# Two transformer layers on one core: weights split once and kept in DRAM as parts, later early maxima, another delay of the row transposes, and normalised outputs in two blocks per chunk

## The chip, the cores and the metric

The kernel runs on one core of a Trainium2 chip. Its engines work side by side: PE (matrix products), DVE (vector work), ACT (functions, and a DMA queue of its own), POOL (slower vector work) and SP (issues most DMAs). The metric is the device time of one execution in microseconds, as a median over runs.

## What is computed

Two equal layers, each an attention block and an MLP with the Mish function, on x of 2048 rows by 512, 32 heads of 16, hidden width 1792. All inputs are float32, and both layers use the same weights.

```python
    def _A_ref(x, wqkv, wo):
        ...
        scores = jnp.einsum("bhqd,bhkd->bhqk", q, k) * (Dh ** -0.5)
        p = _softmax(scores, axis=-1)
        o = jnp.einsum("bhqk,bhkd->bhqd", p, v)
        return (lambda x, *d: x.transpose(*d))(o, 0, 2, 1, 3).reshape(B, S, D) @ wo
    def _B_ref(x, w1, b1, w2):
        h = jnp.einsum("bsd,df->bsf", x, w1) + b1
        sp = jnp.log1p(jnp.exp(-jnp.abs(h))) + jnp.where(h > 0, h, jnp.zeros_like(h))  # stable softplus
        act = h * jnp.tanh(sp)
        return jnp.einsum("bsf,fd->bsd", act, w2)
    x = A_x
    x = x + _A_ref(_layernorm(x, axis=-1), A_wqkv, A_wo)
    x = x + _B_ref(_layernorm(x, axis=-1), B_w1, B_b1, B_w2)
    x = x + _A_ref(_layernorm(x, axis=-1), A_wqkv, A_wo)
    x = x + _B_ref(_layernorm(x, axis=-1), B_w1, B_b1, B_w2)
    return x
```

## The kernel before

**Numbers in two parts.** A float32 operand is split into a rounded part (hi, fp32r) and the rest (lo), and each product is three matmuls (mm3, L136 to L141): hi by hi, hi by lo, lo by hi. A weight block of 0.5 MB is loaded as raw float32 and split into a 1 MB tile of both parts (split_load, L104 to L124): the load on SP's queue (L110) or ACT's (L108), the rounding on ACT, POOL or DVE (L114, L116), the subtraction on POOL or DVE (L118). There are 22 such blocks: 6 of wqkv, 2 of wo, 7 of w1, 7 of w2. Each layer loads and splits all of them again.

**Memory.** Most tiles share one pool of 22 blocks of 8 KB per partition (blk): weights, residuals x2, normed inputs, keys ks, queries qs, values va, probabilities p, and the attention's outputs. A pool of small tiles has the tags raw (3 buffers, raw weights and pt), f (2 buffers: xn, ot, hb), he, hr and others. A tile waits until the last reader of what was in its buffer is done.

**Projections** (qkv, L400 to L464). The 2048 rows are four chunks c of 512. An order of 36 units, (m, c), is worked off: 32 of queries and keys (12 matmuls each, result split into pt and written to DRAM as scr by ACT's queue, L446) and four of values (48 matmuls each, vscr). When the units that the first head group needs are through, SP loads ks and qs for it, 24 loads of 128 KB (prep_qk). From the third unit after that (start, L454; the unit of index 12 in layer 0 and 11 in layer 1), 24 steps of early maxima (AHEAD) are interleaved, one behind each unit or each quarter of a value unit.

**Attention** (run, L366 to L391). 512 steps; a step is one key tile of 128 for four heads and 512 queries. Its work is a fixed order per two steps, CYCLE: Q is two heads' scores (PE matmul L322, exponential on ACT L324), X one score and one row maximum (PE L242, DVE L275), M a pair of maxima (DVE L260), v the product with the values (PE L348). Maxima run 24 steps ahead, since a block's maxima are subtracted inside the score matmul by two extra rows of qs. When 16 steps of maxima are complete, DVE folds them (L282), POOL splits the result (nh, L287 and L288), DVE transposes it (L296) and SP carries it through DRAM into qs (max_rows). The transpose is put on a list with a delay (L289), which tick counts down. When the maxima are through (step 488), the order is TAIL. Each Order chains the instructions that it is given on each engine in the order written; what is not chained (weights, heads, loads) is placed by the framework's scheduler.

**Attention's end and boundary.** After each 16 steps ACT copies a block of outputs to ot (L361), and SP writes its sums and rows to DRAM. heads (L466 to L483) normalises a chunk: load the sums, reciprocal on DVE (L470), write it to DRAM spread over the rows (inv), load raw outputs (oraw) and inverses (rall), and multiply: hi on DVE (L480), the same product again on POOL (L481), lo on DVE (L482). It takes four blocks. heads(0) and (1) are hooked into the attention's last steps, (2) and (3) follow it. project (L485 to L496) multiplies with wo, and DVE adds the residual; then comes a layernorm of chunk 0, and the MLP (hid and outp, hid two ahead). wo is split on POOL in the attention's last group; w1 and w2 are loaded and split around the projections.

Of the kernel before, what the change touches and what calls it, by code (L numbers as in the profile page):

```python
# [50 lines left out]
def kernel(ctx: ExitStack, tc: tile.TileContext, x, wqkv, wo, w1, b1, w2, out):  # L51
# [52 lines left out]
    def split_load(src, a, b, name, hi="act", lo="pool", behind=False, later=None):  # L104
        t = b8([P, 2, a, b], F32R, name)
        raw = tmp.tile([P, a, b], F32, tag="raw", name=name + "r", bufs=3)
        if behind:
            tc.keep_in_program_order(nc.scalar.dma_start(raw, src))  # L108
        else:
            nc.sync.dma_start(raw, src)  # L110

        def split():
# [5 lines left out]
            eng.tensor_tensor(t[:, 1], raw, t[:, 0].bitcast(F32), op=ALU.subtract)  # L118

# [6 lines left out]
    def load_cols(w, j, name, **kw):  # L126
        return split_load(w[:, ts(j, 2 * P)].rearrange("(k p) n -> p k n", p=P), KT, 2 * P, name, **kw)

    def load_rows(w, j, name, **kw):
        return split_load(w[ts(j, 2 * P), :].rearrange("(k p) n -> p k n", p=P), 2, w.shape[1], name, **kw)  # L130
# [335 lines left out]
    def heads(att, c):  # L466
# [9 lines left out]
        nc.sync.dma_start(r, inv.rearrange("h d q -> (h d) q").rearrange("(k p) q -> p k q", p=P))  # L476
        oh = b8([P, KT, CW], F32R, f"oh{l}{c}")
        ol = b8([P, KT, CW], F32R, f"ol{l}{c}")
        for k in range(KT):
            nc.vector.tensor_tensor(oh[:, k], o[:, k], r[:, k], op=ALU.mult)  # L480
            nc.gpsimd.tensor_tensor(o[:, k], o[:, k], r[:, k], op=ALU.mult)  # L481
# [195 lines left out]
```

## Time and profile before

| what | us |
|---|---|
| median of 3 runs (lowest, highest) | 3735.68 (3728.65, 3739.83) |
| the profiled execution's time | 3735.5 |
| span of that execution, first to last instruction | 3733.7 |
| busy: PE, DVE, ACT, POOL | 3518.1, 3096.8, 2564.1, 521.5 |
| mean granted clock of PE | 0.973 |
| layer 0: first matmul of the projection with wo, first h matmul of the MLP | 1464.75, 1539.04 |
| layer 1: first h matmul of the MLP | 3401.67 |

A row of a timeline gives start and length in us, engine, line, operation, output and inputs, and in brackets how long the engine stood idle before it and for what. A row of groups gives the count, busy us and mean ns, and the idle time ahead of the group's instructions with what ended it. A row of the busy table gives for a stretch each engine's busy us and count, the granted clock, the DMA engines' busy share and GB/s. Matmul ends are modelled, so a count of matmuls says more of PE's pace than its busy time.

### The profile page before, as it was taken

What the parts mean: (1) busy time and instruction counts of PE and PEld (TensorE: products, weight loads), DVE (VectorE), ACT (ScalarE), POOL (GpSimd) and SP (SyncE); (2) the same over time, 40 slices, a digit from 0 to 9 for tenths busy, and PEclk for the clock granted to TensorE, in tenths of its full rate; (3) what the DMA queues carried; (4) which work ended last, traced back from release to release, by engine and by line L of the source; (5) the groups of instructions that cost most, each with busy time, mean ns of one, the idle gap of its engine ahead of it and who ended that gap; (6) DMA issues with size and microseconds to landing.
All of it is one profiled execution on the core that took longest, in us unless ns stands there. A gap on an engine that the chain in (4) does not pass through costs nothing.

```text
span 3733.7 us, 70993 instructions
## 1 busy us (share of the span) xinstructions
PE 3518.1 (94%) x29056; PEld 1936.2 (52%) x29056; DVE 3096.8 (83%) x4150; ACT 2564.1 (69%) x4787; POOL 521.5 (14%) x465
## 2 busy tenths in 40 slices
PE   5999999999999988799979999999999999887999
PEld 4654444444444434577757444444444444346787
DVE  4679999999999984766646899999999999856555
ACT  2168888888888875244421788888888888742444
POOL 2000000000000002645410000000000000035444
PEclk8999999999999998899989999999999999888999
DMA  6440211202112015100045402112021120151000
GB/s 187 153 107 21 52 23 35 50 8 51 26 32 51 18 29 173 52 12 12 29 136 170 103 9 51 26 32 51 7 51 33 25 52 17 30 173 51 12 12 23
DMA packets 131894, 203.85 MB, mean 55 GB/s; under 512 B 28656, under 2 KB 73712, under 8 KB 123376
## 3 DMA queue, kind: packets, MB, share of 16 engines
q1 hardware_dynamic: 109872, 159.46, 18.3%
q10 hardware_dynamic: 21696, 39.85, 2.9%
q8 instruction: 228, 3.74, 0.4%
q14 instruction: 98, 0.80, 0.1%
HBM read 121.12 MB, written 77.07 MB: 53 GB/s over the span
## 4 chain that ended last, share of the span: by engine, by line
DVE 67%; PE 17%; POOL 5%; DMA 4%; ACT 3%; issue 2%; SPq 0%; ACTq 0%; POOLq 0%; DVEq 0%
DVE mxv L275 29%; DVE mxv L260 28%; PE pv L348 3%; POOL hb L520 2%; PE sp L322 2%; DVE al L521 2%; PE qk L139 1%; POOL hb L517 1%; DVE he L512 1%; PE qk L141 1%; PE qk L140 1%; DVE ah L519 1%; DMA rall<-inv 1%; DVE he L514 1%; PE va L139 1%
## 5 line engine op out<-in xcount | busy, mean ns | idle before, releaser
L324 ACT ACTIVATE p<-sp 128x512 f32<-128x512 f32 x4096 | 2134.1, 599 | 348.0 <-PE pn L242 206.1
L275 DVE TENSOR_REDUCE mxv<-pn 128x1 f32<-128x512 f32 x2048 | 1323.1, 694 | 27.9 <-PE pn L242 27.1
L260 DVE TENSOR_REDUCE mxv<-pm 128x2 f32<-128x1024 f32 x1024 | 1260.9, 1231 | 78.5 <-PE pm L242 78.0
L322 PE MATMUL sp<-qs,ks 50*128 50x512 f32 x4096 | 1298.0, 450 | 27.0 <-ACT p L324 26.7
L348 PE MATMUL pv<-p,va 128*32 128x256 f32 x16384 | 1209.0, 391 | 0.0
L322 PEld LDWEIGHTS sp<-qs,ks 50*128 50x128 f32 x4096 | 573.3, 185 | 745.8 <-ACT p L324 628.3
L242 PE MATMUL pn<-ks,qs 48*128 48x512 f32 x2048 | 825.0, 451 | 70.6 <-DVE mxv L275 53.2
L348 PEld LDWEIGHTS pv<-p,va 128*32 128x32 f32 x16384 | 380.6, 109 | 555.3 <-issue 441.5
L242 PE MATMUL pm<-ks,qs 48*128 48x512 f32 x2048 | 439.6, 423 | 22.8 <-DMA ks<-scr 16.7
L242 PEld LDWEIGHTS pn<-ks,qs 48*128 48x128 f32 x2048 | 366.9, 184 | 94.9 <-DVE mxv L275 76.6
L287 POOL CAST nh<-nm 128x16 fp32r<-128x16 f32 x64 | 12.7, 198 | 2638.9 <-DVE nm L282 2638.9
L242 PEld LDWEIGHTS pm<-ks,qs 48*128 48x128 f32 x2048 | 195.1, 186 | 86.2 <-DMA ks<-scr 18.0
L139 PE MATMUL mo<-w,ah 128*128 128x512 f32 x448 | 178.7, 399 | 11.0 <-DVE ah L519 7.9
L517 POOL TENSOR_TENSOR hb<-hb,he 128x512 f32<-128x512 f32 x112 | 158.2, 1413 | 183.3 <-DVE he L514 179.1
L521 DVE TENSOR_TENSOR al<-hb,ah 128x512 fp32r<-128x512 f32 x112 | 108.3, 967 | 90.0 <-POOL hb L520 88.8
L520 POOL TENSOR_TENSOR hb<-hb,hr 128x512 f32<-128x512 f32 x112 | 160.8, 1435 | 132.7 <-DVE ah L519 129.4
L139 PE MATMUL h<-thm,w 128*128 128x512 f32 x448 | 177.5, 398 | 1.6 <-ACT thm L133 1.6
L140 PE MATMUL h<-tlm,w 128*128 128x512 f32 x448 | 176.9, 395 | 0.0
L141 PE MATMUL h<-thm,w 128*128 128x512 f32 x448 | 176.8, 395 | 0.0
L140 PE MATMUL mo<-w,ah 128*128 128x512 f32 x448 | 176.2, 393 | 0.0
L515 ACT ACTIVATE hr<-he 128x512 f32<-128x512 f32 x112 | 71.0, 634 | 146.9 <-POOL hb L520 74.3
L133 ACT ACTIVATE pt<-qk 128x512 fp32r<-128x512 f32 x64 | 38.0, 598 | 194.6 <-PE qk L141 185.8
(161 smaller groups left out, 2833.3 us busy)
## 6 DMA issues: line engine op xcount, KB each, us to landing
scr<-pt ACTq DMA_DIRECT2D x64, 512.0 KB
qs<-scr SPq DMA_DIRECT2D x192, 128.0 KB
ks<-scr SPq DMA_DIRECT2D x192, 128.0 KB
vscr<-vst SPq DMA_DIRECT2D x32, 512.0 KB
va<-vscr SPq DMA_DIRECT2D x16, 1024.0 KB
raw<-ot SPq DMA_DIRECT2D x256, 32.0 KB
inv<-sums SPq DMA_DIRECT2D x8, 1024.0 KB
oraw<-raw SPq DMA_DIRECT2D x8, 1024.0 KB
```

What stands on the lines that cost most here:

```text
L139: pe(nc.tensor.matmul(acc, ah, bh, start=first and i == 0, stop=False))
L140: pe(nc.tensor.matmul(acc, ah, bl, start=False, stop=False))
L141: pe(nc.tensor.matmul(acc, al, bh, start=False, stop=last and i == n - 1))
L242: nc.tensor.matmul(out, qs[h // 2][rows, q0 : q0 + P], ks[h // 2][rows, ts(c, 512)], start=True, stop=True)
L260: self.order(nc.vector.tensor_reduce(self.mxs[b][:, 0:2, qt, c], pm, axis=AX.X, op=ALU.max))
L275: self.order(nc.vector.tensor_reduce(self.mxs[b][:, h, qt, c : c + 1], pm, axis=AX.X, op=ALU.max))
L322: nc.tensor.matmul(sp, ks[h // 2][rows, ts(kt, P)], qs[h // 2][rows, ts(qb, CW)], start=True, stop=True)
L324: return lambda: self.order(nc.scalar.activation(self.pts[s][:, h], sp, AF.Exp, scale=SCALE))
L348: nc.tensor.matmul(acc[ts(h, VW), cols], va[:, kt, h, :], self.pts[s][:, h, cols], start=kt == 0 and half == 0, stop=kt == NKT - 1, skip_g ...
L517: nc.gpsimd.tensor_tensor(hb, hb, e, op=ALU.mult)
L520: nc.gpsimd.tensor_tensor(hb, hb, r, op=ALU.mult)
L521: nc.vector.tensor_tensor(al, hb, ah.bitcast(F32), op=ALU.subtract)
```

## The change

1. **Weights.** In layer 0 a weight is loaded raw and split once (make), and both parts, 1 MB, are then written to DRAM by ACT's queue. The six of wqkv are split when they are used; the 16 of wo, w1 and w2 on POOL at hooks 24 steps apart in layer 0's attention. Later uses load the parts (fetch), 1 MB on SP's queue and no split.
2. **Early maxima** start at the unit of index 36 − 22 = 14 in both layers.
3. **Row transposes** get a delay of 2 ticks where it was 1.
4. **heads** takes two blocks per chunk: raw outputs are loaded into ol's, inverses into oh's, and the products go through on, a tile of tag f. Products are on DVE and POOL in turn; rounding and subtraction on DVE. Hooks of heads, residuals and the first w1 move to earlier steps, chunks 0 and 1 are projected before the norm of chunk 0, 2 and 3 after it.

```diff
+MAX_UNITS = 22
...
+    def make(kind, j, hi="pool", lo="pool", later=None):
+        src, a, b = view(kind, j)
+        t = b8([P, 2, a, b], F32R, f"{kind}m{j}")
+        raw = tmp.tile([P, a, b], F32, tag="raw", name=f"{kind}r{j}", bufs=3)
+        nc.sync.dma_start(raw, src)
+        wparts[kind, j] = dram.tile([P, 2, a, b], F32, name=f"{kind}p{j}")
...
             eng.tensor_tensor(t[:, 1], raw, t[:, 0].bitcast(F32), op=ALU.subtract)
+            nc.scalar.dma_start(wparts[kind, j], t.bitcast(F32))
...
+    def fetch(kind, j, name):
+        _, a, b = view(kind, j)
+        t = b8([P, 2, a, b], F32R, name)
+        nc.sync.dma_start(t.bitcast(F32), wparts[kind, j])
+        return t
...
-            self.later.append((1, lambda: self.max_rows(b, nh)))
+            self.later.append((2, lambda: self.max_rows(b, nh)))
...
+            wts[j] = make(kind, i, hi="act", **kw) if l == 0 else fetch(kind, i, f"{kind}{l}{i}")
...
-                        start = i + 3
+                        start = len(order) - MAX_UNITS
...
-        o = b8([P, KT, CW], F32, f"oraw{l}{c}")
-        r = b8([P, KT, CW], F32, f"rall{l}{c}")
+        ol = b8([P, KT, CW], F32R, f"ol{l}{c}")
+        oh = b8([P, KT, CW], F32R, f"oh{l}{c}")
+        o, r = ol.bitcast(F32), oh.bitcast(F32)
...
-        oh = b8([P, KT, CW], F32R, f"oh{l}{c}")
-        ol = b8([P, KT, CW], F32R, f"ol{l}{c}")
         for k in range(KT):
-            nc.vector.tensor_tensor(oh[:, k], o[:, k], r[:, k], op=ALU.mult)
-            nc.gpsimd.tensor_tensor(o[:, k], o[:, k], r[:, k], op=ALU.mult)
-            nc.vector.tensor_tensor(ol[:, k], o[:, k], oh[:, k].bitcast(F32), op=ALU.subtract)
+            on = t512("f", f"on{l}{c}{k}")
+            (nc.gpsimd if k % 2 else nc.vector).tensor_tensor(on, o[:, k], r[:, k], op=ALU.mult)
+            nc.vector.tensor_copy(oh[:, k], on)
+            nc.vector.tensor_tensor(ol[:, k], on, r[:, k], op=ALU.subtract)
...
+        if l == 0:
+            todo = [("wo", i) for i in range(2)] + [("w1", i) for i in range(7)] + [("w2", i) for i in range(7)]
+            for n, (kind, i) in enumerate(todo):
+                hooks[30 + 24 * n] = lambda kind=kind, i=i: make(kind, i)
         for i in range(2):
-            hooks[STEPS - GSTEPS + 2 * i] = lambda i=i: wot.append(load_rows(wo, i, f"wo{l}{i}", hi="pool"))
-            hooks[STEPS - 20 + i] = lambda i=i: load_res(i)
-        hooks[STEPS - 18] = lambda: behind(0)
-        hooks[STEPS - 12] = lambda: behind(1)
+            hooks[STEPS - GSTEPS + 2 * i + 1] = lambda i=i: load_wo(i)
+            hooks[STEPS - GSTEPS + 2 * i + 5] = lambda i=i: load_res(i)
+            hooks[STEPS - 9 + i] = lambda i=i: load_w1(i)
+        hooks[STEPS - 24] = lambda: behind(0)
+        hooks[STEPS - 16] = lambda: behind(1)
+        hooks[STEPS - 4] = lambda: behind(2)
         att.run(hooks)
...
+        behind(3)
+        for i in range(2, 4):
+            load_res(i)
+        for i in range(2, 7):
+            load_w1(i)
+        project(l, 0, parts.pop(0), wot, x2s[0])
+        project(l, 1, parts.pop(1), wot, x2s[1])
+        norm(x2s[0], f"m{l}0", tts, 0, "acc")
+        for i in range(4):
+            load_w2(i)
+        project(l, 2, parts.pop(2), wot, x2s[2])
+        project(l, 3, parts.pop(3), wot, x2s[3])
+        for i in range(4, 7):
+            load_w2(i)
```

Where instructions stand is shown by three pieces of the engines' queues, each of before and of the changed kernel. First DVE's queue in the middle of layer 0's attention, about the fold of block 19; mxv holds maxima, nm the folded ones, nt the transposed. Before:

```order
L275 TENSOR_REDUCE mxv019_10710<-pn0640_11208 128x1
L260 TENSOR_REDUCE mxv019_10710<-pm0320_11212 128x2
L282 TENSOR_REDUCE nm019_11216<-mxv019_10710 128x16
L296 STREAM_TRANSPOSE nt019_11221<-nh019_11218 128x32
L275 TENSOR_REDUCE mxv020_11245<-pn0641_11246 128x1
L275 TENSOR_REDUCE mxv020_11245<-pn0642_11252 128x1
```

In the changed kernel, at the same fold:

```order
L284 TENSOR_REDUCE mxv019_10799<-pn0640_11297 128x1
L269 TENSOR_REDUCE mxv019_10799<-pm0320_11301 128x2
L291 TENSOR_REDUCE nm019_11305<-mxv019_10799 128x16
L305 STREAM_TRANSPOSE nt019_11317<-nh019_11307 128x32
L284 TENSOR_REDUCE mxv020_11341<-pn0641_11342 128x1
L284 TENSOR_REDUCE mxv020_11341<-pn0642_11348 128x1
```

Nothing moved here: the transpose stands directly behind the fold in both. Second, PE's queue in layer 0's projections, where the first early maxima (pm01) begin; qk0 with m and c is a unit's result. Before:

```order
L139 MATMUL qk005_596<-thq00_121,wqk02_92 128x512
L140 MATMUL qk005_596<-tlq00_122,wqk02_92 128x512
L141 MATMUL qk005_596<-thq00_121,wqk02_92 128x512
L242 MATMUL pm01_613<-ks000_529,qs000_530 128x512 x2
L242 MATMUL pn01_617<-ks001_545,qs001_546 128x512
L242 MATMUL pn02_620<-ks001_545,qs001_546 128x512
L139 MATMUL qk015_624<-thq01_185,wqk02_92 128x512
```

And in the changed kernel:

```order
L148 MATMUL qk025_642<-thq02_247,qkm2_93 128x512
L149 MATMUL qk025_642<-tlq02_248,qkm2_93 128x512
L150 MATMUL qk025_642<-thq02_247,qkm2_93 128x512
L251 MATMUL pm01_659<-ks000_541,qs000_542 128x512 x2
L251 MATMUL pn01_663<-ks001_557,qs001_558 128x512
L251 MATMUL pn02_666<-ks001_557,qs001_558 128x512
L148 MATMUL qk035_670<-thq03_299,qkm2_93 128x512
```

The units qk015 and qk025, 12 matmuls each, moved ahead of the first early maxima. Third, ACT's queue at the end of layer 0's attention, with the engines that each instruction waits for; p with its step's number is a tile of probabilities, ot030 and ot031 are the last two output copies. Before:

```order
L324 ACTIVATE p0507_18019<-sp02030_18026 128x512 [waits PE_49]
L324 ACTIVATE p0507_18019<-sp02031_18028 128x512 [waits PE_49]
L324 ACTIVATE p0508_18040<-sp02032_18041 128x512 [waits DMAHW1_49,PE_49,Pool_49]
L324 ACTIVATE p0508_18040<-sp02033_18043 128x512 [waits PE_49]
L324 ACTIVATE p0508_18040<-sp02034_18047 128x512 [waits PE_49]
L324 ACTIVATE p0508_18040<-sp02035_18049 128x512 [waits PE_49]
L324 ACTIVATE p0509_18061<-sp02036_18062 128x512 [waits DMAHW0_49,DVE_49,PE_49]
L324 ACTIVATE p0509_18061<-sp02037_18064 128x512 [waits PE_49]
```

In the changed kernel, from the last step on:

```order
L333 ACTIVATE p0511_18254<-sp02044_18255 128x512 [waits PE_49,Activation_49]
L333 ACTIVATE p0511_18254<-sp02045_18257 128x512 [waits PE_49]
L333 ACTIVATE p0511_18254<-sp02046_18261 128x512 [waits PE_49]
L333 ACTIVATE p0511_18254<-sp02047_18263 128x512 [waits PE_49]
L370 ACTIVATE ot031_18291<-pv031_17964 128x512 [waits DMAHW4_49,DMAHW5_49,DMAHW3_49,DMAHW6_49,DVE_49,DMAHW7_49,PE_49,Pool_49]
L142 ACTIVATE thm00_18463<-tpm000_18467 128x4x128 [waits PE_49]
```

The waits for POOL and DVE went from the first exponentials of p0508 and p0509 to the output copy ot031 (ot030, ahead of p0498, waits for DVE as well); no tile of probabilities of the last steps waits for either engine.

More of the change, by code (lines that the diff above doesn't have):

```diff
@@ L44 @@
 LAG = 2
-BLOCKS = NG * NCH
+MAX_UNITS = 22
 T_BUFS = {"he": 1, "hr": 1}
@@ L102, in t512, with view @@
         return tmp.tile([P, 512], dt, tag=tag, name=name, bufs=T_BUFS.get(tag, 2))
[L104 to L110, printed above, removed]
+    wparts = {}
+    def view(kind, j):
+        if kind in ("w1", "qk"):
+            w = w1 if kind == "w1" else wqkv
+            return w[:, ts(j, 2 * P)].rearrange("(k p) n -> p k n", p=P), KT, 2 * P
+        w = {"w2": w2, "wo": wo, "v": wqkv[:, 2 * D : 3 * D]}[kind]
+        return w[ts(j, 2 * P), :].rearrange("(k p) n -> p k n", p=P), 2, D
+    def make(kind, j, hi="pool", lo="pool", later=None):
[4 more added lines that the diff above has]
+        wparts[kind, j] = dram.tile([P, 2, a, b], F32, name=f"{kind}p{j}")
         def split():
@@ L124, in split_load @@
         return t
[L126 to L130, printed above, removed]
+    def fetch(kind, j, name):
[3 more added lines that the diff above has]
+        return t
     def split_psum(hi, lo, src):
@@ L407, in qkv @@
         chained = False
-        done = 0
+        start = done = 0
         for i, (m, c) in enumerate(order):
@@ L609, in behind, with load_wo @@
             parts[c] = heads(att, c)
-        for i in range(2):
-            hooks[STEPS - GSTEPS + 2 * i] = lambda i=i: wot.append(load_rows(wo, i, f"wo{l}{i}", hi="pool"))
-            hooks[STEPS - 20 + i] = lambda i=i: load_res(i)
-        hooks[STEPS - 18] = lambda: behind(0)
-        hooks[STEPS - 12] = lambda: behind(1)
-        att.run(hooks)
-        for c in range(NCH):
-            if c == 0:
-                behind(2)
-            if c == 1:
-                behind(3)
-            project(l, c, parts.pop(c), wot, x2s[c])
-            if c == 0:
-                for i in range(2):
-                    load_w1(i, hi="pool")
-                load_res(2)
-                load_res(3)
-            if c == 1:
-                for i in range(2, 7):
-                    load_w1(i, hi="dve")
-                for i in range(4):
-                    load_w2(i, hi="dve")
-                norm(x2s[0], f"m{l}0", tts, 0, "acc")
-                for i in range(4, 7):
-                    load_w2(i, behind=True)
+        def load_wo(i):
+            wot.append(fetch("wo", i, f"wo{l}{i}"))
@@ L642 @@
             for f, js in ((2, (0,)), (4, (2,)), (9, (1,)), (11, (3,)), (12, (4,)), (13, (5,))):
-                hooks.setdefault((last, f), []).append(lambda js=js: load_qkv(1, wts, js, behind=True, lo="dve"))
+                hooks.setdefault((last, f), []).append(lambda js=js: load_qkv(1, wts, js))
             for c in range(last):
```

13 lines of the change are left out of this document (5 added, 8 removed).

## The prediction

> **What bounds the kernel now.** I read the page first: its busy times, and the chain that ended last.
>
> ```profile
> PE 3518.1 (94%) x29056; PEld 1936.2 (52%) x29056; DVE 3096.8 (83%) x4150; ACT 2564.1 (69%) x4787; POOL 521.5 (14%) x465
> DVE 67%; PE 17%; POOL 5%; DMA 4%; ACT 3%; issue 2%; SPq 0%; ACTq 0%; POOLq 0%; DVEq 0%
> ```
>
> PE is busy 94%, yet the chain goes through DVE for 67% of the span: in the attention PE spends its slack between matmuls that wait for maxima. The busy table by stage shows it. Columns: length; busy time and count of PE, PEld, DVE, ACT, POOL; granted clock; DMA share; GB/s.
>
> ```profile
> 13.00:20.00 7.00, 4.46 (x13) 3.18 (x14) 6.96 (x14) 3.39 (x5) 4.88 (x3) 1.00 0.89 308
> 66.00:92.00 26.00, 5.54 (x21) 3.58 (x19) 2.61 (x3) 1.20 (x2) 0.00 (x0) 0.61 0.91 192
> 280.00:320.00 40.00, 39.58 (x402) 17.78 (x400) 39.37 (x53) 35.39 (x69) 0.42 (x2) 1.00 0.17 41
> 1240.00:1280.00 40.00, 39.45 (x406) 17.80 (x406) 39.37 (x53) 35.20 (x69) 7.21 (x6) 1.00 0.03 6
> 1440.00:1480.00 40.00, 26.32 (x170) 16.45 (x169) 23.07 (x25) 8.76 (x17) 19.45 (x12) 0.79 0.48 173
> 1919.00:1946.00 27.00, 9.23 (x36) 6.60 (x35) 4.59 (x6) 2.69 (x5) 0.00 (x0) 0.74 0.86 215
> ```
>
> Steady attention (280:320) is DVE at 39.37 of 40 us, ACT at 35.39. There the weights take nothing, so nothing is to be had but by shortening DVE. PE is free in three places per layer: the gap ahead of the attention (5.54 us of work in 26, DMA at 0.91), the attention's end (26.32 of 40), and the start of the MLP. The chain of those places, by PE's timeline with the idle time in brackets, gives the terms:
>
> ```profile
> 76.00 0.79 PE L242 MATMUL pm<-ks,qs 48*128 48x512 f32 x1 [6.36 <-DMA ks<-scr]
> 82.08 0.79 PE L242 MATMUL pm<-ks,qs 48*128 48x512 f32 x1 [5.30 <-DMA qs<-scr]
> 91.69 0.89 PE L242 MATMUL pn<-ks,qs 48*128 48x512 f32 x2 [8.81 <-DMA qs<-scr]
> ...
> 1454.06 0.79 PE L322 MATMUL sp<-qs,ks 50*128 50x512 f32 x1 [12.13 <-ACT p L324]
> ...
> 1464.75 0.50 PE L139 MATMUL wo<-wo,oh 128*128 128x512 f32 x1
> ...
> 1481.71 0.63 PE L141 MATMUL wo<-wo,ol 128*128 128x512 f32 x1
> ...
> 1484.28 0.63 PE L141 MATMUL wo<-wo,ol 128*128 128x512 f32 x1
> ...
> 1539.04 1.62 PE L139 MATMUL h<-thm,w 128*128 128x512 f32 x3 [0.78 <-ACT thm L133]
> ...
> 1933.46 0.76 PE L242 MATMUL pm<-ks,qs 48*128 48x512 f32 x1 [6.76 <-DMA ks<-scr]
> 1937.78 0.76 PE L242 MATMUL pm<-ks,qs 48*128 48x512 f32 x1 [3.56 <-DMA ks<-scr]
> 1947.10 0.89 PE L242 MATMUL pn<-ks,qs 48*128 48x512 f32 x2 [8.55 <-DMA qs<-scr]
> ...
> 3315.05 0.79 PE L322 MATMUL sp<-qs,ks 50*128 50x512 f32 x1 [12.15 <-ACT p L324]
> ```
>
> The last pv matmul is followed by the first wo matmul at 1464.75, and the first h matmul comes at 1539.04: 74.3 us for 192 wo matmuls and the transposes of a norm. At PE's steady pace (44 to 45 starts in 10 us, a row of the MLP below), 0.227 us, they are 43.6 us; behind a wait they start 0.43 us apart (six steps from 1481.71 to 1484.28).
>
> **Attention's end: the block stall.** The waits of 1400 to 1470 name the 12.13 us:
>
> ```profile
> ACT p L324 <- POOL oraw L481: 13.5, 1, 13.5
> ```
>
> A probability tile needs the block that a normalisation on POOL still reads. In the changed order no p tile waits for POOL or DVE at the end, so the stall goes in both layers: 12.1 each. Next late is the last output copy, ot031 on ACT, which the shared "f" buffers put behind heads(2)'s third product on DVE. How long such operations take:
>
> ```profile
> L480 DVE TENSOR_TENSOR oh<-oraw,rall 128x512 fp32r<-128x512 f32 x32 | 37.2, 1223 | 72.5 <-DMA rall<-inv 54.1 <-ACT p L324 18.5
> ```
>
> and a cast of that size or twice it 0.68 us (1502.33, below). heads(2)'s loads stand behind two weight fetches on SP; I put their landing at 1450 (an estimate: issue near 1440, and 7 us for a transfer of 1 MB, from the rows below, with some queueing). Eight DVE operations of 0.68 to 1.22 us follow: 1457.5, where pv would end at 1452.5 (1464.6 − 12.1). I take 1458. ot030 waits likewise for heads(0), 0 to 3 us, while ACT has no slack in the tail; that is within the bounds.
>
> **The boundary.** From that copy on, the old chain is read in SP's issues and, in the second fence, DVE's rows:
>
> ```profile
> 1465.48 0.52 SPq L362 DMA_DIRECT2D rawsum<-ot  x1
> 1469.02 0.45 SPq L469 DMA_DIRECT2D sums<-rawsum  x1
> 1480.44 0.61 SPq L472 DMA_DIRECT2D inv<-sums  x1
> 1487.37 0.36 SPq L476 DMA_DIRECT2D rall<-inv  x1
> ```
>
> ```profile
> 1477.07 3.34 DVE L470 RECIPROCAL sums<-sums 32x512 f32<-32x512 f32 x1 [2.19 <-DMA sums<-rawsum]
> 1494.68 4.63 DVE L480 TENSOR_TENSOR oh<-oraw,rall 128x512 fp32r<-128x512 f32 x4 [4.63 <-DMA rall<-inv]
> 1502.33 0.68 DVE L116 CAST w<-w102r 128x1024 fp32r<-128x1024 f32 x1
> ...
> 1503.53 2.85 DVE L116 CAST w<-w104r 128x1024 fp32r<-128x1024 f32 x1
> ```
>
> The sums took 8.05 us from issue to reciprocal, behind 2 MB of residual loads; those now come after heads(3) in the program, and I take 2.5 us. Then: output copy at 1458, writes of the sums and rows 3.0, sums load 2.5, reciprocal 3.3 (1467); inverse to DRAM 6.9 (1480.44 to 1487.37) and back 7.3 (1487.37 to 1494.68), so 1481; eight DVE operations of about 1.2 us, with the residual adds of projection 1 between them, 13 us, so 1494. What is left on PE is projection 3, 48 matmuls, at the slow 0.43 us 20.6 us, and 3 us of last transposes: h at about 1517.5 instead of 1539. The weight casts on DVE (the row at 1503.53 is one of nine) are gone from here. Stall and boundary together: 21.5 per layer, **−43** for two. The bounds are −39 per layer (below) and −11 (transfers 10 us slower).
>
> **The projections.** PE's order puts two more units ahead of the early maxima in layer 0, three in layer 1: 24 and 36 matmuls at 0.227, 5.4 and 8.2 us of work moved into gaps in which PE waits 20.5 us (6.36 + 5.30 + 8.81) and 18.9 us (6.76 + 3.56 + 8.55). But each moved unit also issues a 0.5 MB write of scr, and in layer 0 two writes of weight parts (1 MB each) stand just ahead of the last write on which the loads wait, on a DMA system that is busy 0.91 at 192 GB/s: 2 MB are 10.9 us there, 1.5 MB at 215 GB/s 7.3 in layer 1. Some of that overlaps SP's own issue time. I take +1 (−5 to +5) in layer 0 and −2 (−8 to +2) in layer 1.
>
> [...] No row here shows ACT's and SP's transfers competing apart from one another.
>
> At the start four part writes of 1 MB (13 to 27 us) meet loads at 0.89 and 308 GB/s: at most 4 MB at 308, 13 us, but the x chunks that follow aren't due before 25 us: +2 (0 to +5).
>
> **The row transposes.** The group says what they cost now:
>
> ```profile
> L296 DVE STREAM_TRANSPOSE nt<-nh 128x32 f32<-128x32 f32 x64 | 13.5, 212 | 38.4 <-POOL nh L288 38.4
> ```
>
> DVE waits 0.6 us 64 times for POOL's split of the folded maxima. A delay of 2 instead of 1 would hide that if it counted cycles. But run calls tick twice at the end of each cycle of two steps, and the fold falls on the cycle's last item: in DVE's order the transpose still stands directly behind the fold in the attention. **0**.
>
> **The splits in layer 0's attention.** Three prices: POOL's cast and subtraction for a weight (ns, least, median, most), and ACT's issue of a DMA (us):
>
> ```profile
> L116 POOL CAST wo<-wo00r x1: 1038/1038/1038, 1267.7 to 1267.7; 128x1024 fp32r<-128x1024 f32 x1
> L118 POOL TENSOR_TENSOR wo<-wo00r,wo x1: 2377/2377/2377, 1268.8 to 1268.8; 128x1024 fp32r<-128x1024 f32 x1
> ```
>
> ```profile
> 59.79 0.37 ACTq L446 DMA_DIRECT2D scr<-pt  x1
> ```
>
> Sixteen times POOL does a cast and a subtraction, 1.04 + 2.38 us, and ACT issues a write, 0.37 us. DVE's maxima do not feel POOL's splits: 39.37 of 40 us both without them (280:320) and with 7.21 us of POOL (1240:1280). ACT's 16 × 0.37 = 5.9 us fit into the 4.6 of 40 us that it has free. Its issue waits for POOL's split, and behind it in ACT's queue stand the exponentials; the split's input is there long before and, as the blocks turn over, some eight steps (20 us) ahead: **+2** (0 to +10).
>
> **The MLP's start and the change of layers.** PE starts fewer matmuls than the 45 in 10 us of its steady pace:
>
> ```profile
> 1549.00:1559.00 10.00, 7.36 (x32) 1.00 0.01 2
> 1569.00:1579.00 10.00, 10.00 (x45) 1.00 0.00 1
> 1880.00:1890.00 10.00, 6.78 (x27) 0.88 0.45 150
> ```
>
> ```profile
> L114 ACT ACTIVATE w<-w204r 128x1024 fp32r<-128x1024 f32 x1 | 1.1, 1060 | 3.1 <-DMA w204r<-in_B_w_dram 3.1
> ```
>
> The first loses 13 matmuls, 3.0 us, where ACT waits for and splits the last three weights (the row is one of them); without that I take −3 per layer (−6 to 0), **−6**. The second loses 18, 4 us, part of it for splits of the next layer's weights on ACT and DVE: **−2** (−5 to 0).
>
> **The sum.** +2 + 1 − 2 + 0 + 2 − 43 − 6 − 2 = −48. The profiled span is 3733.7, so 3685.7; the profiled execution's time stands 1.8 over its span and 0.2 under the median: 3687.5.
>
> **The rivals.**
> (a) The boundary becomes bound by PE: transfers and DVE keep ahead, PE never waits long, and 192 matmuls at 0.227 follow the pv matmuls. 1452.5 + 43.6 + 4 is 1500, −39 per layer; the time is 3687.5 + 43 − 78 = 3652.5. For it: the casts are off DVE. Against it: the round trip of sums and inverse, 14 us, hangs on the last step.
> (b) It is mostly lost: the normalisations now go through the two "f" buffers that the output copies use too, and 14 MB of weight parts are fetched where 7 MB of raw weights were. With transfers 10 us slower h comes at 1528: −11 per layer, 3708.5.
> (c) The transposes do move off the wait: −38.4 more, 3649. The order speaks against it.
> (d) DMA in the projections is additive: at a share of 0.91 every added write lengthens the loads on which the maxima wait, and the work that was moved there only fills what it made. +10.9 and +7.3 instead of +1 and −2, 3706.7. [...]
> (e) ACT's part writes stand before POOL is done: 16 × (1.04 + 2.38 + 0.37) = 61 instead of 2, 3746.5. It decides where the block for a split comes free less than 3.4 us ahead of ACT's issue.
> (f) Slower: the fetch becomes the bound of the MLP's first chunk. From 1441 on, 14 MB of parts, 2 MB of residual and some 4 MB of the last heads have to land before about 1588 (h at 1517, and twelve of its steps of 5.4 us, 24 matmuls at 0.227, then the last w2): 20 MB in 147 us, 136 GB/s. The 1440:1480 row has 173 GB/s at a share of 0.48, which speaks against it. At 110 GB/s it takes 182 us, 35 us late per layer, more than the 21.5 gained: 3687.5 + 70 = 3757.5.
>
> **How the numbers follow.** A measurement here can tell 0.3%, 11.2 us: 3724.5 to 3746.9 is "same". My forecast 0.57, (a) 0.14, (b) 0.13, (c) 0.02, (d) 0.05, (e) 0.04, (f) 0.05. Of (b), 0.03 lies above 3724.5, if its other bounds fall badly too. Faster 0.57 + 0.14 + 0.10 + 0.02 + 0.05 = 0.88; same 0.04 + 0.03 = 0.07; slower 0.05. The range reaches down to (a) and (c), 3648, and up past (b) to 3718, so that (e), (f) and the top of (b), 0.12, and the tails of the forecast stay out.
>
> **What would show it.** Right: no p tile that waits for POOL at either attention's end; h about 21 us earlier there; DVE's wait of 38.4 us for nh unchanged; 39.4 of 40 us of DVE in steady attention, in layer 0 too. Wrong: ACT idle for POOL at its part writes; a wait of ot over 6 us; h matmuls waiting for DMA; the projections' gap longer than before.

## The result and the profile after

| | before | after |
|---|---|---|
| median of runs, us | 3737.76 (3728.65 to 3743.75) | 3647.16 (3641.89 to 3648.58) |
| span of the profiled execution | 3733.7 | 3644.5 |
| mean granted clock of PE | 0.973 | 0.982 |

The ratio is 0.9757 with a 95% interval of 0.9734 to 0.978. The forecast was 3687.5 with 3648 to 3718 as range: the direction was right, the size nearly double, and the time lies 0.8 us below the range. The whole of the engines' work, from the page of the changed kernel:

```profile
PE 3497.0 (96%) x29056; PEld 1925.6 (53%) x29056; DVE 3029.8 (83%) x4142; ACT 2551.7 (70%) x4775; POOL 457.5 (13%) x441
```

PE has the same 29056 matmuls and 21 us less busy time: a matmul's length differed with the clock that PE was granted (in the changed kernel wo matmuls took 0.63 us and started 0.43 us apart from 1473.04 to 1474.75, where the clock was 0.50, and took 0.39 and started 0.227 apart from 1478.21 to 1484.10, where it was 1.00). Where the 89 us went is found by cutting both timelines at the same events: the row transposes of the 2nd, 30th and 32nd fold of each layer (DVE), the first wo and the first h matmul (PE), and the residual adds of the MLP's chunks (DVE). Layer 0 begins at 0, layer 1 at the last chunk's residual adds.

| stretch, us | before, layer 0 / 1 | after, layer 0 / 1 | difference | forecast |
|---|---|---|---|---|
| start to fold 2 | 234.4 / 197.9 | 237.3 / 192.6 | +2.9 / −5.3 | +3 / −2 |
| fold 2 to fold 30 | 1071.7 / 1071.7 | 1071.6 / 1071.6 | −0.1 / −0.1 | +2 / 0 |
| fold 30 to fold 32 | 94.3 / 95.3 | 101.5 / 95.1 | +7.2 / −0.2 | 0 |
| fold 32 to first wo | 64.4 / 64.3 | 49.1 / 49.1 | −15.3 / −15.2 | −21.5 each, |
| first wo to first h | 74.3 / 76.3 | 54.6 / 56.5 | −19.7 / −19.8 | with the row above |
| first h to chunk 0's adds | 100.0 / 99.9 | 90.8 / 90.8 | −9.2 / −9.1 | −3 each |
| rest of the MLP | 257.2 / 226.6 | 250.1 / 227.8 | −7.1 / +1.2 | −2 |

The boundary of layer 0 in PE's timeline of the changed kernel, and behind it ACT's and DVE's rows of the chain that the forecast followed:

```profile
1459.46 0.50 PE L148 MATMUL wo<-wo,oh 128*128 128x512 f32 x1
...
1472.02 0.79 PE L148 MATMUL wo<-wo,oh 128*128 128x512 f32 x1 [4.11 <-DVE x L503]
...
1485.17 0.50 PE L148 MATMUL wo<-wo,oh 128*128 128x512 f32 x1 [0.46 <-DVE x L503]
...
1514.06 0.97 PE L148 MATMUL h<-thm,w 128*128 128x512 f32 x3 [0.69 <-ACT thm L142]
```

```profile
1463.11 0.60 ACT L370 ACTIVATE ot<-pv 128x512 f32<-128x512 f32 x1 [4.89 <-PE wo L150]
```

```profile
1468.08 3.34 DVE L477 RECIPROCAL sums<-sums 32x512 f32<-32x512 f32 x1 [2.52 <-DMA sums<-rawsum]
1471.35 1.21 DVE L503 TENSOR_TENSOR x<-wo,x 128x512 f32<-128x512 f32 x2
...
1483.82 0.69 DVE L487 TENSOR_TENSOR on<-ol,oh 128x512 f32<-128x512 f32 x1 [2.88 <-DMA oh<-inv]
```

In layer 0 there is one wait over 1 us on PE in the boundary, 4.11, where there were six of up to 5.66, and no stall of 12 us. What PE waits for there is a residual add (1471.35), which stands in DVE's queue behind chunk 3's reciprocal: that one waited 2.52 us for its sums and took 3.34. The copy ot031 waits, as forecast (the profile names the last wo matmul as what came last; the order has DVE and POOL there), and chunk 3's inverses land 24.4 us after the first wo matmul. The busy table of the changed kernel (columns as in the prediction) and two stretches of before that were not shown, the MLP's first 30 us:

```profile
1440.00:1480.00 40.00, 35.89 (x273) 22.05 (x273) 18.81 (x28) 18.40 (x37) 4.19 (x4) 0.96 0.61 184
1480.00:1520.00 40.00, 38.10 (x170) 29.91 (x169) 26.94 (x54) 3.72 (x6) 5.02 (x4) 1.00 0.97 391
1524.00:1534.00 10.00, 10.00 (x46) 8.28 (x45) 6.79 (x8) 5.22 (x8) 5.75 (x5) 1.00 0.00 0
```

```profile
1539.00:1549.00 10.00, 9.96 (x36) 8.13 (x37) 1.96 (x2) 2.70 (x3) 4.28 (x2) 0.81 0.50 156
1559.00:1569.00 10.00, 9.40 (x34) 7.64 (x35) 6.55 (x9) 4.98 (x9) 5.76 (x4) 0.83 0.00 0
```

Before, PE started 36 and 34 matmuls in 10 us there, at a clock of 0.81 and 0.83; now 46 at 1.00. The fetch runs at 391 GB/s and PE does not wait for it. The row transposes:

```profile
L305 DVE STREAM_TRANSPOSE nt<-nh 128x32 f32<-128x32 f32 x64 | 13.5, 211 | 37.1 <-POOL nh L297 37.1
```

37.1 us of waiting instead of 38.4: the delay of 2 did nothing in the attention.

### The profile page after: what moved, and what is told of

The parts are those of the page before. It is cut to its first block, busy times and chain, and to the rows that moved or that the text cites. A ratio compares the mean times of both kernels' runs of the same rounds, so it can differ in the third digit from the quotient of the medians.

```text
span 3644.5 us, 71117 instructions
## 1 busy us (share of the span) xinstructions
PE 3497.0 (96%) x29056; PEld 1925.6 (53%) x29056; DVE 3029.8 (83%) x4142; ACT 2551.7 (70%) x4775; POOL 457.5 (13%) x441
## 4 chain that ended last, share of the span: by engine, by line
DVE 35%; PE 10%; POOL 3%; ACT 2%; DMA 1%; issue 1%; SPq 0%; POOLq 0%; ACTq 0%; DVEq 0%
DVE mxv L284 15%; DVE mxv L269 14%; POOL hb L527 2%; PE pv L357 1%; DVE al L528 1%; PE sp L331 1%; POOL hb L524 1%; DVE he L519 1%; DVE he L521 1%; DVE ah L526 1%; PE qk L148 1%; ACT he L520 1%; PE qk L149 1%; PE qk L150 1%; PE h L149 1%
## 5 line engine op out<-in xcount | busy, mean ns | idle before, releaser
L284 DVE TENSOR_REDUCE mxv<-pn 128x1 f32<-128x512 f32 x2048 | 1305.9, 677 | 33.5 <-PE pn L251 30.8
L269 DVE TENSOR_REDUCE mxv<-pm 128x2 f32<-128x1024 f32 x1024 | 1242.0, 1213 | 67.0 <-PE pm L251 67.0
L251 PEld LDWEIGHTS pm<-ks,qs 48*128 48x128 f32 x2048 | 195.5, 187 | 74.5 <-issue 21.4
L520 ACT ACTIVATE he<-he 128x512 f32<-128x512 f32 x112 | 70.8, 632 | 139.1 <-DVE he L519 139.0
```

Source lines behind the costliest of these rows:

```text
L251: nc.tensor.matmul(out, qs[h // 2][rows, q0 : q0 + P], ks[h // 2][rows, ts(c, 512)], start=True, stop=True)
L269: self.order(nc.vector.tensor_reduce(self.mxs[b][:, 0:2, qt, c], pm, axis=AX.X, op=ALU.max))
L284: self.order(nc.vector.tensor_reduce(self.mxs[b][:, h, qt, c : c + 1], pm, axis=AX.X, op=ALU.max))
```

## The experiments

Theory A: part 4 (two blocks, new order) keeps PE busy at the boundary. Theory B: the splits that left DVE, POOL and ACT carry what was gained beyond the forecast. The first four kernels undo one part each, or repair one. The diffs are excerpts; three dots stand for lines left out.

**Weights raw in both layers** (part 1 undone).

```diff
-        nc.sync.dma_start(t.bitcast(F32), wparts[kind, j])
...
+            nc.sync.dma_start(raw, src)
...
+            (nc.gpsimd if hi == "pool" else nc.vector).tensor_copy(t[:, 0], raw)
...
+        eng.tensor_tensor(t[:, 1], raw, t[:, 0].bitcast(F32), op=ALU.subtract)
```

> The changed kernel with part 1 undone alone: every weight is loaded raw and split again at each use, on the engines that did it before, and no parts are written. Theory A (part 4, the two blocks and the new order of heads and projections, keeps PE busy at the boundary, so its clock stays full there): attention's end and boundary stay near 52 + 56 us per layer, the MLP's first chunk near 91 us, and only the change of layers goes back by 5.7 us: 3647 + 4 to 12, 3651 to 3659. Theory B (the splits that went from DVE, POOL and ACT carry the extra gain): boundary back by 10 to 15 us and first chunk back to 100 us in both layers: 3647 + 40 to 55, 3687 to 3702.

Measured 3670.27 us, ratio to before 0.9822 (0.9807 to 0.9836): 23 us of the gain gone, between the two. By stretch (layer 0 / 1): attention's end 49.1 / 49.1, unchanged; boundary 62.0 / 63.0 where it was 54.6 / 56.5; first chunk 97.6 / 98.0 where it was 90.8; chunk 3 with the change of layers 91.3 where it was 87.3 (before: 93.0).

**Old heads, hooks and projections** (part 4 undone).

```diff
-        ol = b8([P, KT, CW], F32R, f"ol{l}{c}")
-        oh = b8([P, KT, CW], F32R, f"oh{l}{c}")
-        o, r = ol.bitcast(F32), oh.bitcast(F32)
+        o = b8([P, KT, CW], F32, f"oraw{l}{c}")
+        r = b8([P, KT, CW], F32, f"rall{l}{c}")
...
+        oh = b8([P, KT, CW], F32R, f"oh{l}{c}")
+        ol = b8([P, KT, CW], F32R, f"ol{l}{c}")
...
```

The products, the hooks and the order of the projections go back as well.

> The changed kernel with part 4 undone alone: four blocks per chunk, hooks and order of the projections as before, weights still fetched as parts. Theory A: the block stall (12.1 us per layer) and all of the boundary's gain go: 3647 + 60 to 72, 3707 to 3719. Theory B: the stall returns but the boundary keeps most of its gain: 3647 + 24 to 40, 3671 to 3687.

Measured 3677.16 us, 0.9842 (0.9823 to 0.986): theory B's figure. Attention's end is 64.1 / 63.8 again, with the stall; the boundary is 57.2 / 57.2 and the first chunk 92.0 / 92.0. So part 4 carries the attention's end, the weights carry the MLP's start, and the boundary is shortened by either alone (74.3 to 57.2 or 62.0), by both to 54.6. The two are not additive: by these two runs the weights give 61 us without part 4, and part 4 gives 68 without the weights, together 90 (parts 2 and 3 are in both runs).

**Old start of the early maxima** (part 2 undone).

```diff
-                        start = len(order) - MAX_UNITS
+                        start = i + 3
```

> The changed kernel with part 2 undone alone: early maxima from the third unit after the last needed one, index 12 and 11. If the moved work fills the gap: second fold later by some 5 us in layer 1 and by 0 to 5 us in layer 0, 3652 to 3657. If the added transfers lengthen the gap by as much (the contention rival): no difference, 3644 to 3650.

Measured 3647.76 us, 0.9762 (0.9747 to 0.9777): no difference, the figure of the contention rival. But the trace has fold 2 6.5 us later in layer 1 and 1.9 in layer 0, as if the moved work does fill the gap, and folds 30 to 32 of layer 0 4.0 us shorter; what is left, 3 us, is within the runs' spread of 8. So the equal time does not show that contention ate the gain.

**Transposes truly a cycle later.**

```diff
-            self.later.append((2, lambda: self.max_rows(b, nh)))
+            self.later.append((3, lambda: self.max_rows(b, nh)))
```

> The changed kernel with a delay of 3 ticks, so that in the attention the transpose stands behind six more maxima reductions. If DVE's wait for POOL is the only thing between it and its own pace: an interval between folds of 37.67 us instead of 38.27, 60 of them, 3647 - 36, near 3611. If PE or ACT is the next bound right behind DVE, the interval stays above 38.1 and the time above 3637. That delay 2 changed nothing in the attention is read from the interval of before and after, 38.27 both.

Measured 3597.92 us, 0.9623 (0.9607 to 0.9639), 49 us better than the changed kernel. Two successive transposes on DVE, first of the changed kernel, then of this one:

```profile
313.80 0.21 DVE L305 STREAM_TRANSPOSE nt<-nh 128x32 f32<-128x32 f32 x1 [0.60 <-POOL nh L297]
352.07 0.21 DVE L305 STREAM_TRANSPOSE nt<-nh 128x32 f32<-128x32 f32 x1 [0.60 <-POOL nh L297]
```

```profile
317.90 0.20 DVE L305 STREAM_TRANSPOSE nt<-nh 128x32 f32<-128x32 f32 x1
355.48 0.20 DVE L305 STREAM_TRANSPOSE nt<-nh 128x32 f32<-128x32 f32 x1
```

37.58 us from fold to fold instead of 38.27: the wait is gone, and 0.09 more. So DVE set the pace, and no other engine held it back within these 0.69 us. The time is 13 us below the 3611 expected. In the profiled execution, which is 44 us shorter, folds 2 to 30 give 19.3 us per layer and folds 30 to 32, for which two waits of 0.60 us were counted per layer, give 10.4 and 5.0, while the starts take some 5 us longer.

**Reciprocals behind the maxima.** The reciprocals of chunks 0 and 1 stand among the last maxima on DVE, and each makes DVE wait for the load of the sums besides:

```profile
1336.03 3.34 DVE L477 RECIPROCAL sums<-sums 32x512 f32<-32x512 f32 x1 [3.70 <-DMA sums<-rawsum]
```

```diff
-        nc.vector.reciprocal(sums, sums)
+        att.order(nc.vector.reciprocal(sums, sums))
```

> The changed kernel with the reciprocals chained behind the maxima on DVE, so that those of chunks 0 and 1 no longer stand among the last maxima. The two intervals between folds 30 and 32 are then 76.5 us where they are 101.5 in layer 0 and 95.1 in layer 1: 43.5 us. If nothing else is late: 3647 - 43 = 3604; the output copy before the last block may wait up to 5 us per layer for heads(0): 3604 to 3614. Rival: what they delayed is needed later anyway (ACT or PE bound the tail): 3630 or more.

Measured 3630.86 us, 0.972 (0.9706 to 0.9735), the rival's figure. Folds 30 to 32 take 76.5 us in both layers, as expected, but attention's end went from 49.1 to 57.0 / 57.6 and the boundary from 54.6 / 56.5 to 61.2 / 61.3. The waits of ACT from 1360 to 1460 show one cause:

```profile
ACT ot L370 <- POOL on L487: 11.4, 1, 11.4
ACT ot L370 <- issue: 6.4, 1, 6.4
```

The output copies wait for heads through the two f buffers: the rival that the forecast priced at 5 us does exist once heads comes later.

**Inverses carried twice.** One more pass of chunk 3's inverses through DRAM.

```diff
+        if c == NCH - 1:
+            again = dram.tile([H, DH, CW], F32, name=f"again{l}{c}")
+            nc.sync.dma_start(again, inv)
+            inv = again
```

> The changed kernel with chunk 3's inverses copied once more through DRAM (1 MB read and written) ahead of their load: its round trip is some 6 to 10 us longer, the work is the same. If the boundary hangs on that chain and PE's idle time costs it its full clock besides: h is later by more than the chain, 9 to 13 us per layer, 3665 to 3673. If the boundary is bound by PE with a slack of 5 us or more: up to 4 us per layer, 3647 to 3655.

Measured 3658.35 us, 0.9792 (0.9777 to 0.9807), between the two. The pass added 5.1 us, less than I took:

```profile
1488.41 0.69 DVE L491 TENSOR_TENSOR on<-ol,oh 128x512 f32<-128x512 f32 x1 [3.45 <-DMA oh<-again]
```

That is 29.5 us after the first wo matmul (1458.91) where it was 24.4; h came 3.4 us later in layer 0 and 2.6 in layer 1. So 5 us on the chain cost some 3: the boundary hangs on chunk 3's round trip with 2 us of cover. The place is DVE's queue: the residual add for which PE waits stands behind these products, and PE's wait there, 0.46 us in the changed kernel, is 2.55.

**Late reciprocals and late transposes together** (the two edits above).

> The changed kernel with the reciprocals chained behind the maxima and a delay of 3 ticks for the row transposes. If the two gains are independent: 3598 - 43 + up to 8 for the next late output copy, 3555 to 3567. If PE or ACT bounds the last two blocks of maxima: 3575 or more.

Measured 3588.03 us, 0.9604 (0.959 to 0.9619): the second figure, but not for its reason. Folds 30 to 32 take 71.2 us, so neither PE nor ACT holds them up, but attention's end and boundary, both layers together, give back 18 and 10 us of it.

**Raw weights, rounding on ACT** instead of DVE (the diff is against the kernel with raw weights).

```diff
-            w1t.append(fetch("w1", i, f"w1{l}{i}", hi="pool" if i < 2 else "dve"))
+            w1t.append(fetch("w1", i, f"w1{l}{i}", hi="pool" if i < 2 else "act"))
...
-            w2t.append(fetch("w2", i, f"w2{l}{i}", hi="dve" if i < 4 else "act", behind=i >= 4))
+            w2t.append(fetch("w2", i, f"w2{l}{i}", hi="act", behind=i >= 4))
```

> The kernel with raw weights in both layers (the first experiment), but the rounding of w1 and w2 around the boundary on ACT instead of DVE (the first two of w1 on POOL as before). If the casts on DVE are what the weights cost at the boundary (they stand between the residual adds for which PE waits): boundary from 62 back to 55 us, 3670 - 14 = 3656 or less. If it is the loads or POOL's subtractions: 3666 to 3674.

Measured 3652.89 us, 0.9778 (0.9759 to 0.9796): the figure of the first theory, at another place than it said. The boundary stayed at 60.4 / 62.3; the first chunk of the MLP went from 97.6 / 98.0 to 90.8 / 91.2. DVE's groups in the second 10 us of that chunk, rounding on DVE (first fence) and on ACT:

```profile
L529 DVE SCALAR_TENSOR_TENSOR he<-he 128x512 f32<-128x512 f32 x2 | 3.4, 1707 | 2.4 <-ACT he L528 2.4
L534 DVE TENSOR_TENSOR ah<-hb,hr 128x512 fp32r<-128x512 f32 x2 | 3.0, 1492 | 3.5 <-ACT hr L531 2.3 <-POOL hb L532 1.2
```

```profile
L529 DVE SCALAR_TENSOR_TENSOR he<-he 128x512 f32<-128x512 f32 x3 | 2.1, 692 | 1.0 <-ACT he L528 0.8
L534 DVE TENSOR_TENSOR ah<-hb,hr 128x512 fp32r<-128x512 f32 x2 | 1.4, 680 | 0.0
```

With the rounding on DVE, POOL's subtractions of the last weights reach into the MLP, and the same DVE operation takes 1707 and 1492 ns on average instead of 692 and 680. One of the pairs behind the first fence:

```profile
1529.67 2.38 POOL L146 TENSOR_TENSOR w<-w206r,w 128x1024 fp32r<-128x1024 f32 x1 [0.26 <-ACT w L142]
1530.30 2.29 DVE L534 TENSOR_TENSOR ah<-hb,hr 128x512 fp32r<-128x512 f32 x1 [2.33 <-ACT hr L531]
```

The DVE operation starts 0.63 us after POOL's and ends 0.54 us after it; that the one lengthens the other is my reading, which no run tests apart. What the weights cost at the boundary, some 6 us, is not settled by this run: the loads and POOL's subtractions, in whose queue the products of heads stand, are both left.

**Products in other buffers.** on in the tag of raw weights, without the f buffers.

```diff
-            on = t512("f", f"on{l}{c}{k}")
+            on = tmp.tile([P, 2, CW], F32, tag="raw", name=f"on{l}{c}{k}", bufs=3)[:, 0]
```

> The changed kernel with the products of heads (on) in the tag of three 4 KB buffers that the raw weights and pt use, free at that time, instead of the two of tag f that the output copies use. The copy ot031 then no longer waits for heads(2): in the changed kernel ACT waits 4.9 us before it. If the boundary hangs on that chain: 4 us per layer earlier, 3647 - 8 = 3639. If PE's work bounds it to within 2 us (as the doubled inverse says): up to 2 us per layer, 3643 to 3647.

Measured 3635.81 us, 0.9735 (0.9721 to 0.975): 11 us, more than either. The copy waits 1.38 us instead of 4.89, and the inverses land 21.4 us after the first wo matmul (1452.44) instead of 24.4:

```profile
1452.57 0.60 ACT L370 ACTIVATE ot<-pv 128x512 f32<-128x512 f32 x1 [1.38 <-PE pv L357]
```

```profile
1473.83 2.36 DVE L487 TENSOR_TENSOR on<-ol,oh 128x512 f32<-128x512 f32 x2 [3.70 <-DMA oh<-inv]
```

The boundary is 49.4 / 51.2, 5 us less per layer. So tying the products to the f buffers did cost. How much of the 5 us is ot031's wait (3.5 us shorter) and how much the third buffer for the products themselves, this run does not separate.

**All three edits together**: late reciprocals, delay 3, on in the raw tag.

> The changed kernel with late reciprocals, a delay of 3 ticks and on in the raw tag. With late reciprocals the output copies waited 6.4 and 11.4 us for heads through the two f buffers. If that sharing is what took back half of the reciprocals' gain: attention's end from 57.5 back to about 50 us and the boundary from 61 to about 56 in both layers, 3588 - 24 = 3564, with 3556 to 3572 as bounds. If it is heads(0) and (1) coming too late for the projections: 3580 or more.

Measured 3588.06 us, 0.9606 (0.959 to 0.9622): no gain over the two without the buffers. Attention's end is 49.2 as expected, but the boundary 67.4 / 66.2. The reciprocals on DVE and the first wait of the projection on PE:

```profile
1363.36 3.30 DVE L477 RECIPROCAL sums<-sums 32x512 f32<-32x512 f32 x1
1383.84 3.33 DVE L477 RECIPROCAL sums<-sums 32x512 f32<-32x512 f32 x1
1404.88 3.33 DVE L477 RECIPROCAL sums<-sums 32x512 f32<-32x512 f32 x1
1435.87 3.32 DVE L477 RECIPROCAL sums<-sums 32x512 f32<-32x512 f32 x1
```

```profile
1435.06 0.80 PE L148 MATMUL wo<-wo,oh 128*128 128x512 f32 x1 [16.93 <-DVE x L503]
```

From a reciprocal to the landing of its inverses it takes 18 to 22 us (the first products of chunks 0 to 2 start at 1381.54, 1401.58 and 1427.10). The next chunk's sums stand behind that on SP, and its reciprocal behind these products on DVE: started together the round trips come one after another, and with the sharing removed the wait only moved to the residual adds. My reading of the run with late reciprocals alone was half the truth.

**Early sums.** The sums of chunks 0 and 1 are loaded six steps ahead of their reciprocals, which are chained at a fixed place on DVE; delay 3, on in the raw tag.

```diff
+        for i, s in enumerate((STEPS - 42, STEPS - 26)):
+            hooks[s] = lambda i=i: early_sums(i)
+            hooks[s + 6] = lambda i=i: early_inverse(i)
...
```

> The changed kernel with a delay of 3 ticks, on in the raw tag, and for chunks 0 and 1 the load of the sums six steps ahead of the reciprocal, which is chained between maxima (chunk 0) or behind the last fold (chunk 1). DVE then spends 3.3 us on one reciprocal among the maxima and waits for no load; folds 30 to 32 take 71.2 + 3.3 = 74.5 us, where they take 90 with the delay of 3 ticks alone; attention's end 49 us, boundary 50 to 52 as with on in the raw tag. 3598 - 2 x 16 - 2 x 4 = 3558, with 3550 to 3566 as bounds. Rival: the four round trips of the inverses pile up as they did when all reciprocals came late, the boundary goes to 60 us or more and the time to 3575 or more.

Measured 3567.41 us (3566.54 to 3569.08), 0.9543 (0.9527 to 0.956): the fastest kernel of this study, 80 us below the changed one, 1.4 us above the bounds. DVE no longer waits at the reciprocal:

```profile
1340.96 3.33 DVE L479 RECIPROCAL sums<-sums 32x512 f32<-32x512 f32 x1
```

Folds 30 to 32 take 75.7 / 75.7, attention's end 49.1 / 49.1, the boundary 49.9 / 51.0; the first chunk, 93.2 / 93.1, is 2.4 us longer than in the changed kernel; why is open.

**The stall filled, twice.** Whether the granted clock is what a stall costs besides its length was tried on the kernel with the old heads. 46 matmuls whose result is not used stand on PE ahead of the scores that wait; first of 48 rows like the maxima's, then of 128 rows.

```diff
+                if s == STEPS - 4:
+                    ks, qs = self.qk[NG - 1]
+                    dummy = pwide(f"dummy{self.l}")
+                    for _ in range(46):
+                        self.order(
+                            nc.tensor.matmul(
+                                dummy[:, 0], qs[0][0:KROWS, 0:P], ks[0][0:KROWS, 0:512], start=True, stop=True
+                            )
+                        )
...
```

> The kernel with the old heads (second experiment), in which the block stall of 11.7 us stands, and 46 added matmuls of the maxima's shape, whose result nobody reads, on PE ahead of the scores that wait: they fill some 10 us of the stall. If the stall costs more than its length because the granted clock has fallen to 0.5 while PE idled: the clock stays at 1.0 and the stretch from the last fold to the last product is 3 us shorter, 61 us where it was 64.1 and 63.8, and the time some 6 us less, 3671. If the extra 3 us have another cause: 64 us or more, and the time 3677 or more.

Measured 3683.12 us, 0.9861 (0.9845 to 0.9878), with 66.7 / 67.8 for the stretch (fold 32 to first wo, 49.1 without a stall): the filler took 16.3 / 16.8 us instead of 10 and the clock fell under it. Layer 0, where the filler stands from 1440.55 to 1456.84:

```profile
1440.00:1445.00 5.00, 5.00 (x31) 3.75 (x24) 0.00 (x0) 1.04 (x3) 0.00 (x0) 0.99 1.04 392
1445.00:1450.00 5.00, 5.00 (x13) 3.80 (x13) 3.12 (x4) 0.00 (x0) 2.21 (x2) 0.50 1.02 398
```

PE never idled there and was granted 0.50. As a test of the theory this run says nothing. The second filler, as a diff against the first:

```diff
-                                dummy[:, 0], qs[0][0:KROWS, 0:P], ks[0][0:KROWS, 0:512], start=True, stop=True
+                                dummy[:, 0], self.wot[0][:, 0, 0, 0:P], self.wot[0][:, 0, 0], start=True, stop=True
...
```

> As the filled stall before, but the 46 added matmuls use all 128 rows of the array (128x128 by 512, wo's tile by itself), as the matmuls of the projections do, at which the granted clock was 1.0. If a stall costs more than its length through the granted clock: the clock stays at 1.0 in the filler and behind it, 0.23 us from start to start, and the stretch from the last fold to the last product is about 61 us where it was 64.1 and 63.8 with the bare stall; time 3671 where that kernel took 3677. If the filler of 48 rows was slowed by something that has nothing to do with rows in use, it falls to 0.5 again within 5 us, and the stretch is 66 us or more. If the clock is full and the stretch still 64: the extra 3 us have another cause.

Measured 3675.41 us, 0.9843 (0.9823 to 0.9864). The filler takes 10.7 us in both layers, and the two differ behind it. In layer 1 the clock stayed at 1.00 through filler and tail, and the stretch is 61.0 (bare stall 63.8); in layer 0 it stayed at 1.00 in the filler, fell to 0.50 at the short waits behind it (1.43 and 0.48 us), and the stretch is 63.5 (64.1). Layer 0's filler and tail, then layer 1's tail, and last that of the bare stall in layer 1:

```profile
1450.00:1455.00 5.00, 5.00 (x25) 3.80 (x23) 5.00 (x5) 0.00 (x0) 4.14 (x3) 1.00 0.68 265
1460.00:1465.00 5.00, 5.00 (x37) 1.69 (x36) 0.00 (x0) 3.43 (x8) 0.00 (x0) 0.50 0.00 0
...
3277.00:3282.00 5.00, 4.02 (x35) 1.86 (x39) 1.57 (x3) 4.88 (x11) 0.00 (x0) 1.00 0.00 0
```

```profile
3281.00:3286.00 5.00, 4.82 (x30) 1.88 (x33) 5.00 (x6) 3.43 (x8) 3.90 (x3) 0.50 0.00 0
```

So the low clock costs about 2.8 us at the attention's end, once the stall itself is paid; that is one layer of one execution. The time, 2 us below the kernel without filler and 4 above the 3671 expected, is within the runs' spread; layer 0's boundary, 59.1 us where it was 57.2, took back what its tail gave.

## Why the prediction was right and wrong

**Right.** The stall for blocks went in both layers. The row transposes gained nothing, and rival (c) was truly excluded by the order alone. Splits and part writes in layer 0's attention cost nothing that the trace shows (+2 forecast, −0.1 measured over 28 folds), so rival (e) falls. Start and projections are +2.9 and −5.3 for +3 and −2; rival (d) falls with layer 1 (−5.3 where it had +7.3). The fetch bound nothing (391 GB/s), so (f) falls. ot031 waited as described.

**Wrong: the sizes at the boundary.** Attention's end and boundary gave 35.0 us per layer instead of 21.5. Three terms of the sum were mis-sized. First, the stall was taken at its length, 12.1; it gave 15.3. The clock in it and behind it, before:

```profile
1452.00:1454.00 2.00, 0.00 (x0) 0.00 (x0) 2.00 (x3) 0.59 (x2) 1.38 (x1) 0.50 0.00 0
1458.00:1460.00 2.00, 2.00 (x16) 0.90 (x16) 1.70 (x2) 1.00 (x3) 2.00 (x2) 0.50 0.00 0
1462.00:1464.00 2.00, 2.00 (x42) 1.22 (x38) 0.00 (x0) 1.72 (x4) 2.00 (x3) 1.00 0.00 0
```

PE started 16 matmuls in 2 us at 0.50 and 42, not all of the same kind, at 1.00; the filled stall shows some 2.8 us for the low clock, of the 3.2. Second, chunk 3's inverses landed 24.4 us after the last product where the forecast had 28.5: the copy waited 3.7 us instead of 5.5, and the way back of the inverses took 5.4 us (1478.38 issued by SP, 1483.82) instead of 7.3. Third, and largest, the last leg: "48 matmuls, at the slow 0.43 us 20.6 us", with 13 us for DVE ahead and 3 behind, made 36.5 us from the landing to h. It was 30.2, and the errors go both ways:

```profile
1491.88 1.28 DVE L489 TENSOR_TENSOR ol<-on,oh 128x512 fp32r<-128x512 f32 x2
```

```profile
1501.27 0.48 PE L148 MATMUL wo<-wo,oh 128*128 128x512 f32 x1
```

DVE had chunk 3's last product ready after 9.4 us, at 1493.16. "What is left on PE is projection 3" did not hold: PE was still at projection 2 and came to projection 3 only 8.1 us later, a term that the sum lacks. The 48 matmuls then took 11.7 us and the rest 1.1. The pace of 0.43 had been read from a stretch of before at half clock, behind a wait of 2.37 us; in the changed kernel PE's waits on this leg are under 0.7 us and the clock is 1.00. Before, and the changed kernel:

```profile
1482.00:1484.00 2.00, 2.00 (x6) 1.52 (x6) 1.63 (x6) 0.00 (x0) 0.29 (x1) 0.50 0.98 210
```

```profile
1484.00:1514.00 30.00, 28.17 (x128) 21.98 (x126) 24.22 (x48) 2.39 (x4) 4.94 (x4) 1.00 1.02 415
```

3.2, 4.1 and 6.3 make up the 13.5 that were missing. So the forecast's path, chunk 3's round trip and then DVE, bounds the boundary up to about the wait of 4.11 us; behind it PE's own work does, with some 2 us to spare on the path. That is the mechanism of rival (a), which was given 0.14, but its 39 us per layer were not reached. That the time comes within 6 us of its 3652.5 is partly luck: the boundary gave 8 us less than (a) has and folds 30 to 32 cost 7, while the MLP and the change of layers gave 16 more than the sum. (The sum's own last step is 0.2 us short, 3687.7; nothing hangs on it.)

**Wrong: the MLP's start and the change of layers.** −3 per layer was taken from one stretch of 10 us; the loss stood in all three (36, 32 and 34 matmuls where 45 is the pace, the first and last with a clock of 0.81 and 0.83), and −9.2 came. The weights' splits are the cause: with raw weights it was −2, and with their rounding on ACT, which lets POOL finish earlier, −9 again. −2 for the change of layers was −5.8 (93.0 to 87.3 in chunk 3), by the same part.

**Missed: folds 30 to 32 of layer 0**, +7.2. DVE's order there is the same and its waits nearly so; PE waits 6.75 and 6.22 us for it before, 6.46 and 6.89 after. PE's clock is not the same, over the stretch behind the first reciprocal, before and after:

```profile
1333.00:1353.00 20.00, 15.53 (x143) 6.91 (x143) 17.71 (x20) 10.96 (x21) 0.23 (x2) 0.83 0.25 54
```

```profile
1336.00:1359.00 23.00, 19.03 (x141) 7.93 (x143) 18.02 (x20) 11.03 (x21) 0.20 (x1) 0.64 0.21 46
```

Nearly the same wait was followed by a longer stretch of low clock. Over these two folds PE's mean clock is 0.91 before (94.3 us), 0.86 with the old start (97.4) and 0.83 in the changed kernel (101.5); without a wait for the sums (early sums) both layers take 75.7. Why the clock stayed low longer is open. The heads are not excluded: the four traces with the old heads have 93.7 to 95.5 us there in layer 0, the six with the new ones, a delay of 2 and the reciprocals not chained 95.3 to 101.5.

## What to carry to other kernels

Price a stall by its length and the matmuls behind it at the clock that they will then have, not at the one that the trace before shows: here a stall of 12.1 us gave 15.3 when it went, and two edits that each remove waits from the same stretch did not add, 61 and 68 us making 90 together. A delay that is counted in calls is read from the order, not from its number: here a 2 did nothing and a 3 gave 49 us. When a chain ends in front of an engine, ask what that engine still has to do then: here it was 8 us of projection 2. And when several round trips are late together, look for the queue in which they stand one behind another before removing the wait that the profile names.
